# Squares over two score steps, score buffers as rows of one tile, and another order of the opening, in an attention and expert kernel on one core

## The chip, the core and the metric

The kernel runs on one core of a Trainium2 chip. The core has a matrix engine (TensorE: PE in the profile, its weight loads PEld), VectorE (DVE), ScalarE (ACT), GpSimd (POOL) and SyncE (SP), each with its own queue of instructions, taken in order; semaphores make one wait for another, and transfers run on 16 DMA engines. The metric is the time of one execution on the chip in microseconds.

## The reference

Attention without softmax over 8 batches, 12 heads, 448 positions and 64 columns a head, then a two-layer expert over the 3584 rows of 768 columns:

```python
scores = (1 / sqrt(64)) * q @ k.transpose(0, 1, 3, 2)
attn   = maximum(scores, 0) ** 2 / 448
x      = (attn @ v).transpose(0, 2, 1, 3).reshape(3584, 768)
h      = x @ w_in                                  # 768 -> 2048
out    = (0.5 * h * (1 + erf(h / sqrt(2)))) @ w_out    # 2048 -> 768
```

All arguments and the result are fp32. The kernel multiplies in bf16 and sums in fp32.

## The kernel before

**Stages of a batch.** The 12 heads of a batch are three groups g of four. Natural-layout loads (`add_k`, `add_q`, `add_v`, issued on POOL, L602, L511, L620, into `nk`, `nq`, `v_sb`) turn fp32 into bf16 on the way. Then K and Q are transposed into `kT` and `qT`: in batches 0 and 1 by TensorE through PSUM (L673 and the Q transposes beside it, with copies L563 on VectorE or L565 on ScalarE), from batch 2 on by DMA transposes issued on SP (`turn` in `add_T_dma`, L739). For each Q group a further step, the swap, writes it a second time with its two halves of partitions exchanged. The attention of one group takes seven *score steps* of 64 keys (`add_steps`): eight products of 64x64 tiles into a PSUM bank `ps` (L816); the relu with the scale into a bf16 buffer `a_sq` of 2 x 448 columns, on ScalarE (L828) or VectorE (L830); and the square, in place, on VectorE (L838). For the first group of batch 0 a score step covers half of the query columns of two key blocks, so it too has up to 896 columns, and the odd blocks at the end have 448. After seven squares comes the *attention product* (`add_av`, 28 products, L878, into `pav`), whose two halves are copied to `xT` by VectorE or ScalarE (L563, L565). The expert follows: six products into `psh` (L937, `add_f1`, the "expert product" of the text below), Gelu on ScalarE into `h_sb` (L947), and second-layer products, from batch 2 on mostly in a Strassen-like form whose sums of parts VectorE makes (L1089, L1120, L1266).

**Buffers.** The score buffers come from `apool`, a pool of `NA = 14` buffers; later in the kernel the same pool holds the fp32 parts of the Strassen-like form. PSUM has three banks of two for `ps` and `pav` (`banks`, class `Banks`) and two for `psh` and transposes (`f_pp`). `h_sb` is one tile, a ring for two batches, which is written and read in parts.

**The order.** A planner adds each operation with its engines, its dependencies and planned durations; its number is the order of its addition. Which engine takes it and in which place is written out by hand in the string `ORDER`. A word is a letter and a number: P is TensorE, A ScalarE, D VectorE, G GpSimd, S SyncE; `Z1056` is a filler of 1056 columns on TensorE, products with zeros that nobody reads. Each engine executes its words in the order of the string, whatever the others do. Since an engine takes its queue in order, an instruction that waits holds everything behind it.

**The opening.** Batch 0's group 0 is loaded first, by two fp32 loads from the ScalarE queue and one from SP's; `spin` and the filler keep TensorE at work until the data land. Then TensorE transposes and multiplies, and ScalarE and VectorE empty its banks, up to about 25 us, while batch 1's transposes and scores are mixed in.

**Holds.** POOL issues the loads, in the order of its queue. Between them stand *holds* (`add_gate`, L784): small POOL copies that read 16 columns of a transposed Q, so that POOL, and the loads behind it, waits until that transpose, or for batch 2 its swap, is done. There is one for each group of each batch from 2 to 6; the one of batch 2, group 1 is word `G224`:

```python
    def add_gate(b, g):
        def fn(e):
            nc.gpsimd.tensor_copy(gate, q_seg(b, 2 * g + (b == 2))[:, : SEG : SEG // 16])

        deps = [Tq[b, g, 0][b == 2]]
        pool_q.append(sch.add((("POOL", 0.2, 0.3),), fn, deps))
```

`qT` of batch b and of batch b + 2 lie in the same place, so a transpose for batch 4 may only be issued once batch 2's readers, the hold among them, are through.

Of the kernel before, what the change touches and what calls it, by code (L numbers as in the profile page):

```python
# [16 lines left out]
HS = S // 2  # L17
KB = 64
NK = S // KB
NA = 14  # L20
NN = 4
# [73 lines left out]
P127 A58 A102 D91 P129 P143 D94 D100 D103 P158 A144 A159 P104 A105 A106 G132 P146 D130 D147 D128  # L95
S213 P229 P170 P182 D183 G9 A230 P155 A171 D154 A156 P227 G114 P140 A141 D160 P194 P164 D165 A195
A228 P237 P149 P173 G131 P200 G134 P239 A238 P241 D145 A150 A201 A174 D148 D157 A240 P176 A177 D151
D142 D172 P161 D184 A162 A242 D166 P179 P167 P235 P233 D175 D178 D163 D180 P197 P206 G118 A168 A236
D169 A198 D181 A234 P185 D207 P203 A186 P188 P231 A187 A232 P243 D214 G221 P247 A244 S212 A248 D202
D204 P249 A250 P245 D189 A246 P257 P272 D199 D205 P191 P269 D192 A258 A273 A270 G117 P255 A256 D190  # L100
G138 P251 P266 D196 D193 S215 P275 A276 D208 S216 D267 A252 P209 A210 P281 P284 A211 P356 P340 A282
G133 D217 D285 P290 P305 P308 D291 D292 A357 P342 G137 G260 A341 A309 P344 G259 G136 D283 D306 A343
A345 P253 P299 P293 P278 D268 D286 D279 D280 D271 A254 P350 A351 P352 A353 P358 A359 S219 D220 P346
A347 D300 D301 D277 P362 A363 P366 P364 P302 D294 S218 D274 D295 P317 D303 P287 A318 A367 P329 P296
A365 A288 D310 A330 D304 D307 D289 D297 P360 A361 P354 A355 G222 P370 G223 G225 G261 P326 S389 D390
P314 A315 P332 D333 A327 P372 P323 S388 P320 G262 A321 G264 A371 D380 D298 P311 P439 S392 D324 D328
D322 D381 P430 P368 D383 A373 D384 A312 D334 D313 D316 A369 P348 A349 P338 A431 A339 P377 D382 A378
D385 A440 P411 S395 A412 G139 P445 D387 G226 A446 D325 D441 D407 G399 D386 P436 D331 D408 P433 P374
A375 A437 A434 P415 G263 G403 D393 D409 S391 P413 P457 P460 A461 S379 D319 D414 P335 P442 D458 P451
A336 A416 A452 P417 P419 D459 A443 A337 S394 D432 D396 D447 D418 D410 P454 P463 D420 P427 A428 P421  # L110
P423 P475 G265 D435 D553 D438 A455 A464 D429 P466 D444 G398 P448 D424 A476 D467 D422 G400 D456 G405
P478 P484 P521 G404 G397 G402 G224 A485 D479 D462 D468 D477 A449 P525 D465 D453 A522 S532 A450 P469
P481 D533 A526 P487 A488 A470 P511 A482 S531 P517 P493 D471 P490 S538 P472 D494 D495 D483 S535 A491
A512 G540 D473 G401 A518 D474 P606 P594 P529 A607 A595 P519 A530 P597 P591 P603 A520 P527 D551 D552
D489 A604 D480 D605 A528 G545 P501 A502 P513 A514 D592 D608 D598 S534 P505 A506 G542 P507 P600 D492
D593 P609 D486 P496 A610 D536 A508 A497 D601 G406 A498 P627 P630 D631 P523 A628 D602 A524 S537 S539
P615 P618 P633 P503 P509 D632 A619 G548 D611 A634 A504 D635 P515 D629 A510 D596 P499 P621 D599 A616
S376 A500 A622 P624 G541 D625 P612 A516 A613 S696 D620 P657 D614 D617 D626 P645 A658 S702 G550 P555
A646 A556 G544 D554 S426 S695 P557 P559 D697 S425 D623 P757 S699 G710 P639 P636 A758 D640 G547 P648
D558 A560 P760 D637 A761 P561 A638 P563 D641 D562 G708 D700 G705 D659 P654 A649 D650 G706 P772 P651  # L120
A773 D564 D571 A655 P565 A652 D566 D573 D572 P567 D568 P766 P754 P642 A643 A767 D656 G546 G549 S698
G709 P575 D653 D644 P577 P769 D774 D768 D647 S701 A576 A755 P778 A779 D770 D762 P660 P763 G712 P790
A764 A661 A791 P579 D578 S569 P581 D756 P787 P793 D771 D574 A580 A662 P796 A794 A797 D582 D765 D780
D792 A788 P583 S703 D759 D584 D789 P585 P808 G543 G707 S827 P802 A803 P775 P784 S829 G842 D809 P781
D586 P587 P669 S826 D795 D828 A782 D783 G837 A776 A777 D798 A785 D714 A670 P805 S830 P814 A815 D786
D806 S833 P799 P811 D810 D588 P817 S831 S570 D800 D801 D804 P667 A818 P671 A812 A668 P870 A871 D807
P867 P873 D816 D874 A868 P677 A672 P876 P820 P864 D819 A678 P691 A692 A877 P689 G711 P673 D875 D872
D821 D715 G838 S832 P891 D813 A865 D822 D892 G840 G713 P894 P823 A690 P879 D824 A895 A674 D896 P900
A880 P665 A825 D834 P663 G843 G839 D866 A901 G835 G836 G704 P882 P888 A666 D869 A664 P903 A889 A883
P683 S937 S940 A684 D893 P687 P693 P927 D717 D878 A904 S942 P897 D881 D884 A928 P885 P906 D898 A688  # L130
A694 S943 D907 P921 P679 S941 S590 A680 P685 S939 D899 D716 P681 A686 P675 A922 A682 D908 D902 A676
P718 D905 P918 A886 A887 P912 D890 P909 D919 P924 A913 D938 S936 P930 P720 D914 A719 D923 P722 A931
D925 A910 P915 P964 S589 A911 P952 D721 D926 D723 P724 A965 P726 D932 P985 D953 D920 D725 A916 D944
P946 P988 A947 D727 D734 P728 A986 A989 D735 D929 D917 P730 G841 P961 P955 D731 S733 D729 P933 A962
D736 P958 A956 A959 P738 D963 D934 A935 P949 A950 D737 P1009 P994 D960 D954 D948 D957 A739 P740
P742 D741 S732 D990 A995 A1010 G945 P744 P973 D951 D1028 D966 D996 D1011 P1006 A1007 A743 D745
D1026 D1018 P967 P997 A974 A998 P746 D846 D968 D1021 A969 D747 P748 P976 D749 D1027 A977 P982 P979
A980 A983 P750 D978 D844 P848 P970 D751 P1003 D845 P1000 P850 D981 D987 D999 A849 P852 D1008 D851
P854 A1004 D984 A1001 D975 P1012 A971 D972 D1005 S752 D1029 D1118 D1002 A1013 A853 D1014 P991 D855
D1022 D1023 P1015 D1019 D847 A992 A993 P856 A1016 A1017 P1064 A1065 D1324 P858 P1081 A1082 P1066  # L140
P1030 P1047 A1048 D1230 D1025 D1067 D1024 D1119 D1121 P1032 P1085 P1051 A1086 D857 A1052 P1070
P1049 P1068 D1231 A1069 A1031 P1055 D1050 D1033 P1053 D1054 D1071 D1020 P1072 D1073 P860 P1034
A1035 P1058 D1059 P1075 D859 P1156 P1036 P1078 D1056 P1061 D1076 D1322 D1062 D1037 P1122 P1083
A1157 P1160 A1123 A1161 P1089 D1079 D1084 D1232 D1120 P1041 D1042 P1158 A1074 P1038 A1080 P1087
P1139 A1077 P1126 A1127 A1140 D1039 D1088 D1090 A1091 D1159 P1092 P1095 P1173 A1060 A1174 P1162
A1043 D1093 P1044 D1045 P1124 D1096 D1125 D1163 P1177 P1143 A1097 A1057 A1046 A1178 P1141 D1142
P1128 P1130 P1175 S862 A1094 A1040 D1129 P1145 P1167 D1176 S753 D1131 A1144 D1168 P1179 A1063 D1098
P1285 A1169 D1146 P1147 D1148 P1136 D1180 D861 P1150 D1151 P1102 P1133 D1134 P1184 D1099 D1137
D1100 D1185 P1164 D1165 P1153 P1181 P1104 P1234 A1132 D1154 A1286 A1149 A1103 D1105 D1182 A1186
P1268 P1106 P1170 P1108 A1107 A1152 P1110 D1109 D1171 D1101 D1111 S863 A1235 P1289 P1187 A1135  # L150
D1190 D1191 A1166 D1188 P1251 P1114 D1115 S1117 A1183 A1252 P1255 P1112 A1172 P1194 P1253 P1236
D1113 A1138 A1269 P1272 D1193 D1192 A1155 D1237 A1189 A1290 A1273 P1196 D1254 P1238 P1287 P1240
D1195 P1198 A1239 D1197 D1199 P1200 P1270 D1233 D1288 D1271 D1201 A1256 P1293 P1257 P1291 P1242
P1202 D1258 D1241 P1274 D1243 D1292 P1296 D1203 P1245 P1248 P1204 D1249 D1246 D1294 D1275 P1262
D1205 P1326 D1210 P1276 D1297 A1298 A1327 D1211 P1206 P1279 D1280 D1277 D1212 D1207 P1259 P1330
D1260 P1214 P1282 P1299 D1300 P1216 P1377 S1209 A1215 D1323 D1263 P1328 D1329 P1360 A1247 D1217
P1265 A1295 A1361 A1264 P1332 P1218 D1266 D1283 A1219 A1284 S1116 D1325 D1213 A1278 P1220 A1281
P1334 P1222 D1221 D1223 P1224 P1364 P1226 A1331 A1267 D1225 A1301 P1306 P1362 D1304 D1302 D1303
D1333 P1337 D1227 P1379 D1335 P1340 A1378 D1363 D1380 A1307 A1244 P1366 P1310 D1341 D1338 P1383
# [272 lines left out]
def kernel(  # L432
# [366 lines left out]
    def add_steps(todo, bias=0.0, dve=False):  # L799
        for blocks in todo:  # L800
# [58 lines left out]
            for blk in blocks:  # L859
                if blk[2] == NK - 1:  # L860
                    add_av(blk, bias)
# [777 lines left out]
```

## Time and profile before

| | |
|---|---|
| three runs | 364.56, 364.74 and 364.97 us, median 364.74 |
| profiled execution, its span | 364.6 us |
| TensorE busy | 354.6 us, 97% |
| VectorE busy | 297.8 us, 82% |
| ScalarE busy | 205.5 us, 56% |
| GpSimd busy | 67.0 us, 18% |
| granted TensorE clock in the slices of the span | 9 tenths or more in all of them |

The profile is of one execution. Its own time and its span are the same 364.6 us, as there is one core and the span runs from its first to its last instruction; the runs have their median 0.1 us above that. In a group of instructions the columns are line, engine, operation, output and inputs by the program's names, shapes, count, then busy time and mean duration, then the idle time of the engine just before them and what ended most of it. A line of a timeline has the start, the length, the engine and the work, with the idle time before it in brackets.

### The profile page before, as it was taken

What the parts mean: (1) busy time and instruction counts of PE and PEld (TensorE: products, weight loads), DVE (VectorE), ACT (ScalarE), POOL (GpSimd) and SP (SyncE); (2) the same over time, 40 slices, a digit from 0 to 9 for tenths busy, and PEclk for the clock granted to TensorE, in tenths of its full rate; (3) what the DMA queues carried; (4) which work ended last, traced back from release to release, by engine and by line L of the source; (5) the groups of instructions that cost most, each with busy time, mean ns of one, the idle gap of its engine ahead of it and who ended that gap; (6) DMA issues with size and microseconds to landing.
All of it is one profiled execution on the core that took longest, in us unless ns stands there. A gap on an engine that the chain in (4) does not pass through costs nothing.

```text
span 364.6 us, 8274 instructions
## 1 busy us (share of the span) xinstructions
PE 354.6 (97%) x3439; PEld 222.0 (61%) x3439; DVE 297.8 (82%) x510; ACT 205.5 (56%) x333; POOL 67.0 (18%) x102
## 2 busy tenths in 40 slices
PE   8799999999999899999999999999999999999995
PEld 4464544555544455554455555899977887787663
DVE  3999878869999779999977999987866576767764
ACT  4999665546678585777966766425634025235000
POOL 8666173111723024052000000000000000000000
PEclk9999999999999999999999999999999999999999
DMA  9999999999899999999955301020101002402324
GB/s 175 201 200 200 184 172 178 191 197 207 134 173 177 144 232 166 196 173 224 192 132 72 91 2 45 2 62 27 42 6 43 2 8 80 131 0 61 99 58 131
DMA packets 72085, 43.87 MB, mean 120 GB/s; under 512 B 36336, under 2 KB 68720, under 8 KB 72048
## 3 DMA queue, kind: packets, MB, share of 16 engines
q0 software_dynamic: 32032, 22.47, 42.8%
q1 hardware_dynamic: 39120, 20.03, 28.6%
q10 hardware_dynamic: 896, 0.85, 0.7%
q8 instruction: 27, 0.44, 0.5%
q14 instruction: 10, 0.08, 0.1%
HBM read 45.61 MB, written 11.01 MB: 155 GB/s over the span
## 4 chain that ended last, share of the span: by engine, by line
PE 63%; DMA 21%; DVE 5%; ACT 4%; issue 3%; POOL 2%; SPq 0%; POOLq 0%; DVEq 0%
PE pso L1266 27%; PE pb L1089 18%; DMA nq<-in_q_dram 9%; PE psh L937 7%; DMA qT<-nq 7%; PE ps L816 5%; PE pav L878 4%; ACT a_sq L828 4%; DMA kT<-nk 4%; DVE a_sq L838 2%; DMA nk<-in_k_dram 2%; PE spin L1445 1%; DVE osb L1300 1%; DVE qT L563 1%; POOL wout_sb L532 1%
## 5 line engine op out<-in xcount | busy, mean ns | idle before, releaser
L828 ACT ACTIVATE a_sq<-ps 128x896 bf16<-128x896 f32 x126 | 110.5, 925 | 36.5 <-PE ps L816 36.2
L838 DVE TENSOR_TENSOR a_sq<-a_sq 128x896 bf16<-128x896 bf16 x169 | 96.4, 615 | 2.0 <-ACT a_sq L828 1.6
L937 PE MATMUL psh<-xT,win_sb 128*128 128x448 bf16 x384 | 76.9, 353 | 0.0
L830 DVE TENSOR_SCALAR a_sq<-ps 128x896 bf16<-128x896 f32 (+1 forms) x43 | 46.2, 1076 | 15.9 <-PE ps L816 15.6
L937 PEld LDWEIGHTS <-win_sb 128*128 128x128 bf16 x384 | 35.6, 98 | 38.2 <-issue 7.2
L1120 DVE TENSOR_TENSOR part<-pb,part 128x448 f32<-128x448 f32 x80 | 46.9, 619 | 12.9 <-PE pb L1089 11.1
L1266 PEld LDWEIGHTS <-s_sb 128*128 128x128 bf16 x424 | 40.4, 98 | 27.1 <-issue 3.3
L816 PE MATMUL ps<-qT,kT 64*64 64x448 bf16 (+1 forms) x700 | 47.8, 350 | 3.6 <-ACT a_sq L828 1.9
L947 ACT ACTIVATE h_sb<-psh 128x448 bf16<-128x448 f32 x64 | 34.5, 549 | 19.5 <-PE psh L937 19.5
L1266 PEld LDWEIGHTS <-h_sb 128*128 128x128 bf16 x312 | 29.9, 98 | 20.1 <-issue 2.3
L1089 PEld LDWEIGHTS <-win_sb 128*128 128x128 bf16 x384 | 36.9, 98 | 2.2
L1266 PE MATMUL pso<-t_sb,s_sb 128*128 128x384 bf16 x208 | 38.1, 326 | 0.0
L1266 PE MATMUL pso<-wout_sb,h_sb 128*128 128x384 bf16 x208 | 38.1, 326 | 0.0
L1266 PE MATMUL pso<-wout_sb,s_sb 128*128 128x384 bf16 (+1 forms) x208 | 37.7, 324 | 0.2 <-DVE osb L1300 0.2
L878 PE MATMUL pav<-a_sq,v_sb 64*64 64x448 bf16 (+1 forms) x700 | 36.1, 342 | 1.2 <-ACT a_sq L828 0.8
L1132 ACT ACTIVATE h_sb<-part 128x448 bf16<-128x448 f32 x48 | 25.2, 573 | 21.1 <-DVE part L1120 21.1
L816 PEld LDWEIGHTS <-kT 64*64 64x64 bf16 x700 | 18.3, 105 | 26.6 <-issue 18.1
L1300 DVE TENSOR_TENSOR osb<-pso,p_sb 128x384 f32<-128x384 f32 x39 | 21.5, 552 | 13.5 <-PE pso L1266 10.9
L878 PEld LDWEIGHTS <-v_sb 64*64 64x64 bf16 x700 | 20.9, 107 | 12.7 <-issue 2.2
L1089 PEld LDWEIGHTS <-ws 128*128 128x128 bf16 x288 | 27.7, 98 | 1.2
L1089 PE MATMUL pb<-xs,ws 128*128 128x224 bf16 x192 | 22.8, 259 | 0.0
L1089 PE MATMUL pb<-xs,win_sb 128*128 128x224 bf16 x192 | 22.5, 259 | 0.0
(70 smaller groups left out, 311.8 us busy)
## 6 DMA issues: line engine op xcount, KB each, us to landing
nk<-in_k_dram POOLq DMA_DIRECT2D x23, 224.0 KB, 8.1
nq<-in_q_dram POOLq DMA_DIRECT2D x23, 224.0 KB, 8.8
v_sb<-in_v_dram POOLq DMA_DIRECT2D x4, 672.0 KB, 8.9
out_dram<-osb SPq DMA_DIRECT2D x7, 336.0 KB, 3.8
v_sb<-in_v_dram POOLq DMA_DIRECT2D x10, 224.0 KB, 8.0
out_dram<-osb SPq DMA_DIRECT2D x7, 288.0 KB, 2.8
out_dram<-osb SPq DMA_DIRECT2D x8, 240.0 KB, 3.3
win_sb<-in_moe_w_in_dram POOLq DMA_DIRECT2D x8, 192.0 KB, 9.0
```

Source lines behind the costliest of these rows:

```text
L816: nc.tensor.matmul(ps[64 * j : 64 * j + 64, e, x * w : x * w + w], kT[r, g, i * 128 + 64 * j : i * 128 + 64 * j + 64], moving, start=True, ...
L828: A.activation(ar, ps, AF.Relu, scale=c_att)
L830: V.tensor_scalar(ar, ps, c_att, 0.0, op0=mybir.AluOpType.mult, op1=mybir.AluOpType.max,)
L838: V.tensor_mul(box["a2"][:, :, :used], ar, ar)
L878: nc.tensor.matmul(pav[0][o2 : o2 + 64, e, :w], get_v()[r, 2 * v_slot(b, g) + e, bass.ts(i, D)], box["a2"][r, y, o : o + w], start=(i == 0 ...
L937: nc.tensor.matmul(ph[:, x * n : x * n + n], win_sb[:, kd, bass.ts(m + x, 128)], xT[b][:, kd, c], start=(kd == 0), stop=(kd == KD - 1),)
L947: A.activation(h_ring()[:, m : m + nm, o + c.start : o + c.stop], box[0][:, :S].rearrange("p (x n) -> p x n", x=nm), AF.Gelu,)
L1089: nc.tensor.matmul(ps[name][:, z * HS : z * HS + HS], w[:, k, bass.ts(mm, 128)], right()[:, k], start=first and k == 0 and z == 0, stop=k ...
L1120: V.tensor_add(get(to), ps[name][:, :S], get(other))
L1132: A.activation(h_ring()[:, m : m + 2, o + half[c].start : o + half[c].stop], src().rearrange("p (x n) -> p x n", x=2), AF.Gelu,)
L1266: nc.tensor.matmul(box[bank][:, n0:n1], left()[:, kf], right()[:, kf, n0:n1], start=bool(need) and kf == 0, stop=kf == K2 - 1, skip_group_ ...
L1300: V.tensor_add(out()[:, n0:n1], box[bank][:, n0:n1], other()[:, n0:n1])
```

## The change

Four things are changed together.

1. In batches 0 and 1 (`PAIRED = 2`) the score steps of a group are taken in pairs. The two relus write into one buffer of up to 2 x 896 columns, and one square covers both; the seventh step has a square of its own. So a group has four squares in place of seven, and a square waits for two relus.
2. The 14 score buffers are now 14 rows of one tile (`Slots`), handed out when the kernel is built: the row, or pair of rows, that was given back longest ago. A row is given back by the attention product that reads it. For the Strassen-like form the tile is opened anew with rows of fp32.
3. In the written order the hold of batch 2, group 1, moves up on POOL: `G224` before, `G205` now, from behind the load `G402` to a place ahead of the load `G139` (now `G129`).
4. The opening stands in another order, on all engines, and some of its relus and copies change between ScalarE and VectorE; the filler moves from its start to a place between score steps. TensorE's order differs from before up to about the first score steps of batch 4, and is the same from there to the end.

Numbers shift, since paired squares are fewer operations: those behind batch 0's squares are 10 lower, those behind batch 1's 19 lower (`P627` is now `P608`). The order of SP's queue is the same. POOL's differs only in the hold.

```diff
-ORDER = """
-D13 G0 Z1056 A10 G1 G7 G4 A16 G108 G1461 P11 D12 P14 D15 P17 P29 P32 D18 P38 D39 P19 P21 A30 D20
-P35 D22 P27 A33 P62 D31 P77 A36 D40 D28 A63 P59 D34 P44 P25 G2 G3 A78 A60 D37 D45 G111 P121 P65 A66
-P71 A72 P47 P74 A75 D79 A48 D122 D64 D67 P23 D73 P50 D24 D26 P68 G107 P41 A51 P98 A69 D76 A99 D61
-D52 D70 P53 P123 G5 G115 G112 A42 A43 G8 G116 A54 G6 P95 P86 A96 A87 P80 D46 D124 A81 A82 P89 P92
-P119 D55 D97 D49 D90 P125 P83 A93 A84 D120 P56 G109 G110 G113 P152 D126 D88 G135 D85 A57 A153 P101
...
+ORDER = """
+A10 D13 G0 G1 G7 G4 G98 G1442 P11 P14 A16 A15 D12 P17 P31 A18 P29 P19 P34 P21 A30 A20 D32 D35 A22
+P36 P27 P70 P55 D28 D33 A37 A71 A56 P42 P65 P25 P57 D43 G2 G3 A66 A58 G101 P60 Z1056 P44 P62 A45 P23
+P67 G97 D26 D38 D61 A63 A68 P39 P49 P47 G5 G105 G102 A40 A24 A41 A48 D59 D64 D69 D50 D72 D51 D46 G8
+G106 G6 P109 P86 P111 P88 P73 A87 A110 A89 A112 A74 P83 P81 P115 P113 D82 D75 A84 D85 D116 A114 P76
+P78 P91 A77 A79 A92 G99 G100 G103 G125 P145 P119 P117 P140 P52 A146 A141 A53 A54 D80 D90 D93 P94 A95
...
+class Slots:
...
+    def open(self, dtype, size):
+        assert not self.held
+        self.size = size
+        self.tile = self.pool.tile([128, self.n * size], dtype, tag="a", name="a_sq")
+
+    def take(self, k=1, near=0):
+        busy = {y for x, c in self.held.values() for y in range(x, x + c)}
+        runs = []
+        for x in range(0, self.n, k):
+            if not busy & set(range(x, x + k)):
+                alone = near if k == 1 and x ^ 1 not in busy else 0
+                runs.append((alone + max(self.used.get(y, 0) for y in range(x, x + k)), x))
+        x = min(runs)[1]
+        t = self.tile[:, x * self.size : (x + k) * self.size]
...
-    apool = pool("apool", NA)
+    apool = pool("apool", 1)
...
+    slots_a = Slots(apool, NA, 2 * S)
...
+        for _, steps in runs:
+            n = 2 if steps[0][0][0] < PAIRED else 1
+            for x in range(0, len(steps), n):
+                add_pair(steps[x : x + n], bias, dve)
...
-            def fn_relu(e_, box=box, used=used):
-                box["a2"] = apool.tile([128, 2, S], BF16, tag="a", name="a_sq")
-                ar, ps = box["a2"][:, :, :used], box["ps"][:, :, :used]
+            def fn_relu(e_, n=n, used=used, off=off):
+                if "a" not in box:
+                    box["a"] = slots_a.take(len(steps), 6 if steps[0][0][0] < PAIRED else 0)
+                ar = box["a"][:, off : off + 2 * used].rearrange("p (y n) -> p y n", y=2)
+                ps = box["ps", n][:, :, :used]
...
-            def fn_mul(e_, box=box, used=used):
-                ar = box["a2"][:, :, :used]
-                V.tensor_mul(box["a2"][:, :, :used], ar, ar)
...
+        def fn_mul(e_, total=total):
+            ar = box["a"][:, :total]
+            V.tensor_mul(ar, ar, ar)
...
+        o3 = sch.add((("DVE", d, d + 0.12),), fn_mul, relus, bias=bias)
...
+            for box in {id(SQ[x][1]): SQ[x][1] for x in blocks}.values():
+                slots_a.give(box["a"])
...
-                tmp[name] = apool.tile([128, S], F32, tag="a", name="part")
+                if slots_a.size > S:
+                    slots_a.open(F32, S)
+                tmp[name] = slots_a.take()
```

More of the change, by code (lines that the diff above doesn't have):

```diff
@@ L20 @@
 NA = 14
+PAIRED = 2
 NN = 4
@@ L110 @@
[L110 to L119, printed above, removed]
@@ new lines @@
+G106 G6 P109 P86 P111 P88 P73 A87 A110 A89 A112 A74 P83 P81 P115 P113 D82 D75 A84 D85 D116 A114 P76
+P78 P91 A77 A79 A92 G99 G100 G103 G125 P145 P119 P117 P140 P52 A146 A141 A53 A54 D80 D90 D93 P94 A95
+D118 D120 A96 G122 P142 P130 P210 P166 D143 D131 A211 A167 S194 P208 P135 P137 P132 P218 G9 G104
+A133 A209 D144 D168 D136 D147 A138 A219 D134 P156 P151 P220 P222 P177 G121 G124 A152 A157 A178 D139
+P158 P148 P182 A221 A149 D159 D160 D150 A183 A223 P153 P214 P163 P161 P216 A215 D162 D154 A164 A217
@@ new lines @@
+S200 P343 P345 P289 S199 D201 D267 D252 D288 D255 D282 D258 D290 A344 A346 P310 P268 P298 P347 P335
+D299 A269 A348 A270 D311 D300 A336 G203 G204 G206 G242 P295 P313 P307 P351 P341 S370 A314 D285 D291
+D273 D276 D361 A352 A296 A308 A342 S369 P353 P349 P304 P292 G243 G245 G205 A354 A350 D362 D363 D315
+D371 D305 S373 P301 P426 P358 D293 A294 A427 A302 A359 D364 D365 D297 P417 P411 P420 P329 P319 S376
+G129 G207 G380 A412 A330 A320 A418 A421 D306 D309 D366 D303 D368 D413 D312 D367 D374 D388 D389 D377
@@ new lines @@
+P584 P468 P510 P500 A454 D458 D461 D455 D585 D586 D467 A469 A511 A501 G526 P578 P474 P581 P488 P482
+A579 A489 S515 G523 P508 A582 A483 A509 D475 D464 D470 D473 D574 D583 D517 D476 D533 G387 P494 P486
+P575 P608 A495 A487 A609 D576 S518 S520 P477 P611 P590 P504 G529 A591 D478 D612 D613 D610 D592 D534
+D580 A479 A505 P484 P490 P599 P596 P614 A485 A491 P480 P496 A600 A615 D577 D616 A597 D589 P602 S357
+A481 A603 P605 G522 D606 P593 A497 A594 S677 D601 P638 D595 D598 D607 P626 A639 S683 G531 P536 A627
@@ L168 @@
+D1388 A1368 D1395 D1390 A1340 P1391 D1396 D1392 P1399 D1397 S1394 D1400 P1401 P1403 A1357 S1393
+D1398 D1402 D1404 P1405 P1407 D1406 D1408 P1409 D1415 D1417 D1410 P1411 D1416 D1412 P1419 S1414
+D1420 P1421 D1422 P1423 D1424 P1425 S1436 S1413 P1427 D1418 P1433 D1426 D1428 D1431 D1435 S1437
+S1440 P1429 P1432 D1430 S1438 D1434 S1439
 """
@@ L428, in give, with __init__ @@
             self.free.append(self.slot[id(t)][0])
+class Slots:
+    def __init__(self, pool, n, size):
+        self.pool, self.n, self.size = pool, n, size
+        self.used, self.clock, self.held = {}, 0, {}
+        self.open(BF16, size)
+    def open(self, dtype, size):
[11 more added lines that the diff above has]
+        t = self.tile[:, x * self.size : (x + k) * self.size]
+        self.held[id(t)] = (x, k)
+        return t
+    def give(self, t):
+        x, k = self.held.pop(id(t))
+        self.clock += 1
+        for y in range(x, x + k):
+            self.used[y] = self.clock
 @with_exitstack
@@ L799, in add_steps, with add_pair, fn_qk @@
     def add_steps(todo, bias=0.0, dve=False):
+        runs = []
         for blocks in todo:
-            box = {}
+            key = (blocks[0][:2], blocks[0][3])
+            if not runs or runs[-1][0] != key:
+                runs.append((key, []))
+            runs[-1][1].append(blocks)
+        for _, steps in runs:
+            n = 2 if steps[0][0][0] < PAIRED else 1
+            for x in range(0, len(steps), n):
+                add_pair(steps[x : x + n], bias, dve)
+    def add_pair(steps, bias, dve):
+        box, relus, sizes = {}, [], []
+        for n, blocks in enumerate(steps):
             w = S if blocks[0][3] is None else HS
             used = w * len(blocks)
-            def fn_qk(e_, blocks=blocks, box=box, w=w):
-                ps = box["ps"] = banks.take("ps")
+            off = sum(sizes)
+            sizes.append(2 * used)
+            def fn_qk(e_, blocks=blocks, n=n, w=w):
+                ps = box["ps", n] = banks.take("ps")
                 for x, (b, g, i, half) in enumerate(blocks):
@@ L833, in fn_relu @@
                     )
[L834 to L838 removed]
+                banks.give(box["ps", n])
             deps = []
@@ L851, in add_steps @@
             o2 = sch.add(
-                eng, fn_relu, [o1], need=("a",), frees=("w",), bias=bias, other=RELU_DVE
-            )
-            d = 0.07 + used / 960
-            o3 = sch.add((("DVE", d, d + 0.12),), fn_mul, [o2], bias=bias)
-            for x, blk in enumerate(blocks):
-                QK[blk] = o1
-                SQ[blk] = (o3, box, x * w)
-            for blk in blocks:
-                if blk[2] == NK - 1:
-                    add_av(blk, bias)
+                eng, fn_relu, [o1], need=() if n else ("a",) * len(steps), frees=("w",),
+                bias=bias, other=RELU_DVE,
+            )
+            relus.append(o2)
+            for blk in blocks:
+                QK[blk] = o1
+        total = sum(sizes)
+        def fn_mul(e_, total=total):
+            ar = box["a"][:, :total]
+            V.tensor_mul(ar, ar, ar)
+        d = 0.07 + total / 1920
+        o3 = sch.add((("DVE", d, d + 0.12),), fn_mul, relus, bias=bias)
+        for n, blocks in enumerate(steps):
+            w = S if blocks[0][3] is None else HS
+            for x, blk in enumerate(blocks):
+                SQ[blk] = (o3, box, sum(sizes[:n]) + x * w, sizes[n] // 2)
+        for blk in steps[-1]:
+            if blk[2] == NK - 1:
+                add_av(blk, bias)
     def add_av(blk, bias):
@@ L876, in fn @@
                         n, y = (i, e) if b < 2 else divmod(NK * e + i, 2)
-                        _, box, o = SQ[blocks[n]]
+                        _, box, o, used = SQ[blocks[n]]
+                        o += y * used
                         nc.tensor.matmul(
@@ L884, in fn @@
                         )
+            for box in {id(SQ[x][1]): SQ[x][1] for x in blocks}.values():
+                slots_a.give(box["a"])
         deps = list(dict.fromkeys(SQ[x][0] for x in blocks)) + ld_v[b, g]
-        last = {id(SQ[x][1]): x for x in SQ}
-        gone = sum(last[id(SQ[x][1])] == x for x in blocks)
+        gone = sum(len(o.deps) for o in {id(SQ[x][0]): SQ[x][0] for x in blocks}.values())
         d = 7 * 0.19 * w / S
@@ L1138, in fn @@
                     banks.give(ps["a"])
+                if frees == ("a",):
+                    slots_a.give(src())
             d = 0.19 + 0.00069 * S
```

121 lines of the change are left out of this document (56 added, 65 removed).

## The prediction

> **What bounds the kernel now.** I read the page first, then the busy times by stretch, the list of waits, the chain, and last the timelines of single engines. From the page, and from the table of stretches (window, its length, then busy time and count of PE, PEld, DVE, ACT, POOL):
>
> ```profile
> span 364.6 us, 8274 instructions
> PE 354.6 (97%) x3439; PEld 222.0 (61%) x3439; DVE 297.8 (82%) x510; ACT 205.5 (56%) x333; POOL 67.0 (18%) x102
> ...
> 10.00:15.00 5.00, 3.69 (x86) 2.31 (x86) 5.00 (x10) 4.91 (x7) 2.73 (x4) 1.00 1.26 203
> 15.00:20.00 5.00, 3.91 (x79) 2.39 (x82) 4.80 (x10) 5.00 (x10) 3.52 (x5) 1.00 1.39 196
> 20.00:25.00 5.00, 4.84 (x132) 3.64 (x125) 4.98 (x9) 5.00 (x9) 3.66 (x7) 1.00 1.30 200
> 120.00:140.00 20.00, 18.69 (x186) 9.40 (x187) 15.33 (x26) 12.96 (x22) 5.43 (x9) 1.00 1.17 194
> 240.00:300.00 60.00, 60.00 (x542) 51.99 (x540) 45.14 (x82) 21.86 (x46) 0.00 (x0) 1.00 0.09 28
> ```
>
> TensorE sets the end: whoever wants to shorten the run must remove its idle time, and there is little. Two places matter here. From 10 to 25 us TensorE has 2.6 us idle while VectorE and ScalarE are full: the opening is bound by these two, which empty PSUM. Between 120 and 140 us it loses 1.3 us at once. What waits, from the timelines of PE and SP, the waits of SP's queue, and POOL's timeline:
>
> ```profile
> 123.20 1.49 PE L878 MATMUL pav<-a_sq,v_sb 64*64 64x448 bf16 x28
> 126.01 0.57 PE L816 MATMUL ps<-qT,kT 64*64 64x448 bf16 x8 [1.31 <-DMA kT<-nk]
> ...
> 43.78 9.94 SPq L739 DMA_TRANSPOSE qT<-nq  x2
> ...
> 90.01 2.22 SPq L739 DMA_TRANSPOSE kT<-nk  x1
> 97.70 1.31 SPq L739 DMA_TRANSPOSE qT<-nq  x1
> ...
> SPq L739 <- POOL gate L784: 5.3, 1, 5.3
> ...
> 71.53 0.22 POOL L784 COPY gate<-qT 128x16 bf16<-128x16 bf16 x1
> 96.73 0.72 POOL L511 DMA_DIRECT2D nq<-in_q_dram  x1
> 97.45 0.22 POOL L784 COPY gate<-qT 128x16 bf16<-128x16 bf16 x1
> 106.74 0.24 POOL L784 COPY gate<-qT 128x16 bf16<-128x16 bf16 x1 [9.07 <-DMA qT<-nq]
> 107.25 0.70 POOL L602 DMA_DIRECT2D nk<-in_k_dram  x1 [0.27 <-issue]
> ```
>
> At 126.01 the first score step of batch 4, group 1 waits for its transposed K. That K was loaded at 107.25, behind the hold at 106.74 (a hold is the small POOL copy that waits for a transpose, so that the loads behind it wait too), which waited 9.07 us for the Q transpose issued at 97.70. SP was through with the transpose before it at 92.2 (90.01 + 2.22) and then stood 5.3 us for POOL: the new transpose writes over batch 2's Q buffer, which the hold at 97.45 still had to read. That hold is the one for batch 2, group 1, G224 of the order. The chain confirms the leg:
>
> ```profile
> 97.70 8.92 DMA qT<-nq
> 106.76 0.49 issue
> 107.25 5.71 DMA nk<-in_k_dram
> 112.98 12.98 DMA kT<-nk
> 126.01 0.57 PE ps L816 x8
> ```
>
> **The hold that moves.** As G205 it now stands ahead of the load of V of batch 2, group 2 (G129), which ran right before the hold at 71.53, so at about 71 us. It passes eight loads and three holds on POOL; their order is kept. The swap that it waits for belongs to a Q transpose issued from 43.78 on, so it costs the 0.22 us of its copy and saves the same later. SP's next Q transpose then goes at about 92.4. It takes between 5.1 us (another Q transpose, in the fence below) and 8.9 us (its own row), so it lands at 97.5 to 101.3. POOL is busy until 97.45, so the K load leaves between 97.8 and 101.6, 5.6 to 9.4 us before 107.25, and transposed K lands near 117 to 120 if the remaining 18.8 us stay. TensorE needs it at 124.5, as worked out below; so the 1.3 us of idle go, and nothing else of the DMA chain is late next. The later loads move forward too and share the rings; up to 5 us of that are covered.
>
> **The squares.** Batch 0 goes from 22 to 12 squares and batch 1 from 21 to 12: 19 fewer on VectorE. Rows of DVE and ACT, first by shape (busy us, mean ns), then stretches of the timelines (start, length), then two lines of the chain:
>
> ```profile
> L838 DVE TENSOR_TENSOR a_sq<-a_sq 128x896 bf16<-128x896 bf16 x167 | 95.7, 617 | 2.0 <-ACT a_sq L828 1.6
> L830 DVE TENSOR_SCALAR a_sq<-ps 128x896 bf16<-128x896 f32 x42 | 45.5, 1086 | 15.5 <-PE ps L816 15.2
> L1195 DVE TENSOR_TENSOR t_sb<-wout_sb,t_sb 128x1536 bf16<-128x1536 bf16 x4 | 3.7, 954 | 0.0
> L563 DVE COPY kT<-tp 128x896 bf16<-128x896 bf16 x5 | 3.1, 616 | 0.0
> L828 ACT ACTIVATE a_sq<-ps 128x896 bf16<-128x896 f32 x125 | 110.1, 927 | 36.5 <-PE ps L816 36.2
> L828 ACT ACTIVATE a_sq<-ps 128x448 bf16<-128x448 f32 x1 | 0.7, 657 | 0.0
> L565 ACT CAST xT<-pav 128x448 bf16<-128x448 f32 x26 | 13.3, 540 | 0.9 <-PE pav L878 0.6 <-DVE xT L563 0.2
> ...
> 5.90 0.39 PE L673 MATMUL tp<-ident,nk 128*128 128x128 bf16 x4
> ...
> 23.16 3.29 DVE L838 TENSOR_TENSOR a_sq<-a_sq 128x896 bf16<-128x896 bf16 x6
> ...
> 7.32 10.93 ACT L828 ACTIVATE a_sq<-ps 128x896 bf16<-128x896 f32 x13 [1.59 <-PE ps L816]
> 27.16 0.97 ACT L565 CAST xT<-pav 128x448 bf16<-128x448 f32 x2
> ...
> 27.30 1.24 PE psh L937 x6
> ...
> 84.78 5.14 DMA qT<-nq
> ```
>
> Six squares in a row take 3.29 us: one occupies VectorE for (3.29 - 0.617) / 5 = 0.535 us. From 896 to 1536 columns the duration rises by 0.337 us, 0.527 ns a column; 1792 columns make 1.09 us, or 1.01 of occupancy, against 2 x 0.535 = 1.07. A pair saves 0.06 us, 19 pairs 1.1 us, and the ten of the opening 0.6 us. All of it is VectorE's; it reaches the end only where VectorE is last. In return a square waits for both of its relus.
>
> **The opening's other order.** This is what decides. Moved from VectorE to ScalarE: six transposes' copies of 896 columns (A20, A22, A24, A110, A112, A114; before D20, D22, D24, D120, D122, D124), the first two K pieces (A15, A18; 512 and 384 columns) and the 448-column relu A37. Moved the other way: the relus of 896 columns D32, D35, D61, the 448-column D50, and one attention copy (D75). A relu of 896 columns occupies ScalarE for (10.93 - 0.93) / 12 = 0.83 us, a cast of 448 for 0.97 - 0.54 = 0.43, a relu of 448 about 0.5. The trace has no ScalarE copy of a bf16 transpose. Its bounds: 0.43 us if ScalarE took two bf16 elements at a time, as VectorE does (a copy 0.53 us, a relu from f32 1.0), and 0.83 if it takes one, like every ScalarE row there is. I take 0.83. So ScalarE gains 6 x 0.83 + 0.9 + 0.5 = 6.4 us and loses 3 x 0.83 + 0.5 + 0.43 = 3.4, and one batch-1 relu fewer stands ahead of batch 0's last attention copies (0.83): 2.1 us more up to them.
>
> The Trainium skill, "ScalarE: Activation LUTs", section "Step-by-step: what each stage is for", says that ScalarE takes one element per cycle, 0.833 ns, for fp32 and bf16 alike. By it a copy of 896 columns streams in an estimated 0.75 us, six in 4.5 instead of 5.0, and the sum ahead would be 0.5 us less; no row here shows a bf16 source, and the rule speaks against this move, since VectorE does the same copy in 0.53.
>
> ScalarE ran from 7.32 without a real gap to 28.13 (27.16 + 0.97). Its first K copy can now start when the transposes end, 6.3, so 1.0 us earlier, with some 0.2 of new waits before the first score. Batch 0's last copies end 2.1 - 1.0 + 0.2 = 1.3 us later, and with them the first expert products, which fill TensorE from 27.30 on. VectorE is relieved of nine pieces and stands idle meanwhile. Bounds: with 0.43 a copy, 2.4 us less on ScalarE, VectorE becomes the end and the opening is about 0.2 us shorter (its saved squares against waits of about 0.4); with longer waits at the start, 2.0 us longer. After the opening TensorE is full and the delay stays in its queue.
>
> **Smaller edits.** The 1056-column fill moves from 5.13 us into the opening, between score steps: 0.45 us where TensorE waits anyway, 0.45 lost if not. One tile in place of fourteen buffers costs nothing if reads and writes of different rows do not wait for each other: the h_sb ring is written and read by parts in one tile, and its writer waits for its own product alone:
>
> ```profile
> ACT h_sb L947 <- PE psh L937: 19.5, 32, 1.4
> ACT a_sq L828 <- PE ps L816: 36.2, 37, 2.6
> ...
> 126.58 1.24 PE psh L937 x6
> 128.51 4.65 PE psh L937 x24
> ```
>
> The relus wait for scores only, never for a free buffer, so pairs that hold two rows at once have room. Up to the order's P602 (before P621, started 133.09) TensorE does the same work in another sequence, and from there its order is unchanged. The sequence has four more changes between kinds of product: six products alone take 1.24 us, in a row 4.65 / 4 = 1.16, so 4 x 0.08 = 0.3 us. The first step that needs the late K (P608, before P627) now stands ahead of the attention product P477 and one score step, 1.5 us of work: TensorE, free at 126.01 - 1.31 = 124.7 before, reaches it at 124.7 - 1.5 + 1.3 = 124.5.
>
> **Sum**, against the profiled execution's span: 364.6 + 1.3 (opening) - 1.3 (126 us) + 0.3 = 364.9. The three runs have their median at 364.74, 0.1 above this span: 365.0. About 0.2% (0.7 us) is what a measurement can tell from no change.
>
> **Rivals.** *The opening costs nothing* (faster). If ScalarE copies bf16 at double rate, or its extra work lies where it would have waited, the opening is between 0.2 shorter and 0.2 longer, and 126 us pays: 365.0 - 1.3 = 363.7, down to 363.3. For it: ScalarE idles 1.59 us before 7.32, and VectorE has the shorter queue. Against: ScalarE is at 5.00 of 5 us until 25. *The K is still late* (slower). The loads that leave earlier crowd the rings, and K lands at 126 again. TensorE now arrives with 1.5 us of work undone, waits there until 126 as before, and still has it to do, with some 0.2 of the switches: 364.7 + 1.5 + 0.2 = 366.4. It decides from a landing after 124.5 on. For it: that transpose took 12.98 us behind five loads. Against: the chain gains at least 5.6 us. *Rows wait for each other* (the change does not do what it says): if a relu waited for the attention products of other rows, 16 of the 24 products would each stop ScalarE for 1.3 us, over 10 us more. The h_sb row speaks against it.
>
> **Chances.** Forecast 0.54, of which 0.34 within 0.2%, 0.14 slower (opening longer by 2.0 rather than 1.3) and 0.06 faster; opening free 0.22; late K 0.21; rows 0.03. So faster 0.28, same 0.34, slower 0.38. The range runs from the free opening at its best, 363.3, to the late K, 366.4, and leaves out the tails beyond.
>
> **What would show it.** Right: SP's wait for the gate gone, a Q transpose at about 92.4, no wait for kT at the batch-4 step; 24 squares in batches 0 and 1 at about 1.09 us for 1792 columns; ScalarE copies of kT and qT near 0.93 us; the first expert product at 28.6 instead of 27.30, VectorE with idle time before 30. Wrong: ScalarE copies near 0.55 us, the first expert product at or before 27.3, or a kT wait that stays.

## The result, and the profile after

The changed kernel takes 367.06 us (median of 7; 366.69 to 370.78), the kernel before 364.74 (median of 7, same chip): a ratio of 1.0074, interval 1.0051 to 1.0097. It is slower by 2.3 us; forecast were 365.0 and a range up to 366.4.

The spans of these executions are given beside their times, and a time is always 1.7 to 1.9 us more than its span. So the statement above that the profiled execution's time and its span are the same 364.6 us is wrong: with this span it was an execution of some 366.4 us. The profiled execution of the change, 370.78 us, is the slowest of its seven, so a second profile was taken of each kernel. First the page of the change, first profile:

```profile
span 369.0 us, 8260 instructions
PE 355.6 (96%) x3439; PEld 221.7 (60%) x3439; DVE 294.5 (80%) x487; ACT 209.3 (57%) x337; POOL 64.8 (18%) x102
```

VectorE has 3.3 us less and ScalarE 3.8 more to do than before. The table of stretches (window, length, then busy time and count of PE, PEld, DVE, ACT and POOL, granted clock, DMA share, GB/s) of the second profile of before, and of the second of the change:

```profile
core 0 of [0], span 363.6 us
...
10.00:15.00 5.00, 3.88 (x88) 2.36 (x89) 5.00 (x10) 4.91 (x7) 3.18 (x5) 1.00 1.27 204
15.00:20.00 5.00, 3.62 (x84) 2.24 (x79) 5.00 (x11) 5.00 (x9) 2.71 (x5) 1.00 1.36 191
20.00:25.00 5.00, 4.77 (x116) 3.29 (x114) 4.78 (x10) 5.00 (x9) 3.57 (x6) 1.00 1.32 203
```

```profile
core 0 of [0], span 365.1 us
...
10.00:15.00 5.00, 4.00 (x81) 2.56 (x84) 4.67 (x7) 4.97 (x8) 2.41 (x4) 1.00 1.26 203
15.00:20.00 5.00, 4.14 (x114) 2.90 (x107) 5.00 (x7) 5.00 (x9) 3.43 (x5) 1.00 1.38 196
20.00:25.00 5.00, 3.13 (x64) 1.81 (x58) 3.86 (x5) 5.00 (x8) 3.72 (x7) 1.00 1.31 204
```

Between 20 and 25 us TensorE now stands for 1.9 us of the 5, while ScalarE is full and VectorE is not. What it waits for there, from the timelines of PE, ACT and DVE of the change (second profile):

```profile
22.44 1.10 PE L865 MATMUL ps<-qT,kT 64*64 64x448 bf16 x12 [0.20 <-DVE a_sq L881]
24.54 0.38 PE L865 MATMUL ps<-qT,kT 64*64 64x448 bf16 x4 [1.00 <-ACT a_sq L879]
...
18.95 1.04 ACT L599 COPY kT<-tp 128x896 bf16<-128x896 bf16 x1
19.74 1.07 ACT L879 ACTIVATE a_sq<-ps 128x896 bf16<-128x896 f32 x1
20.55 1.06 ACT L599 COPY qT<-tp 128x896 bf16<-128x896 bf16 x1
21.33 0.71 ACT L599 CAST xT<-pav 128x448 bf16<-128x448 f32 x1
21.76 1.11 ACT L879 ACTIVATE a_sq<-ps 128x896 bf16<-128x896 f32 x1
22.57 1.10 ACT L599 COPY kT<-tp 128x896 bf16<-128x896 bf16 x1
23.35 4.38 ACT L879 ACTIVATE a_sq<-ps 128x896 bf16<-128x896 f32 x5
...
25.33 2.63 DVE L910 TENSOR_TENSOR a_sq<-a_sq 128x1792 bf16<-128x1792 bf16 x3 [0.80 <-ACT a_sq L879]
```

Score steps have filled their three banks by 23.5 us; the bank that TensorE wants at 24.5 waits for a relu on ScalarE, and ahead of that relu stand copies of transposed K and Q. VectorE idles 0.8 us for a later relu of the same row of five. The whole way, from the first transposes to the step from which TensorE's order is the same again (P621 before, P602 after), by the first and last rows in PE's timelines, with the first expert product between them, before and after (second profiles):

```profile
6.74 0.37 PE L705 MATMUL tp<-ident,nq 112*128 112x112 bf16 x4
...
28.28 1.31 PE L937 MATMUL psh<-xT,win_sb 128*128 128x448 bf16 x6
...
132.81 0.57 PE L816 MATMUL ps<-qT,kT 64*64 64x448 bf16 x8
```

```profile
5.58 0.37 PE L739 MATMUL tp<-ident,nq 112*128 112x112 bf16 x4 [0.48 <-ACT nq L599]
...
28.80 0.55 PE L998 MATMUL psh<-xT,win_sb 128*128 128x448 bf16 x2
...
134.16 0.57 PE L865 MATMUL ps<-qT,kT 64*64 64x448 bf16 x8
```

That is 126.07 us before and 128.58 after, 2.5 more. Of this, 1.7 lie in the opening, up to the first expert product: 28.28 - 6.74 = 21.5 us before, 28.80 - 5.58 = 23.2 after. It is 21.5 in each trace with the opening of before, apart from the one with a moved copy, and 23.2 in each trace of the change with its own opening. Behind the first expert product the two run the same products, TensorE never stands idle in either trace, and the change takes 0.8 us more, so the sequence alone costs that: 104.53 us in all five traces with TensorE's order of before and no wait there, 105.36 to 105.37 in three with that of the change. Leaving out the filler, TensorE's order changes 71 times between transposes, attention and expert products on the whole way, before 59 times; behind the first expert product it changes 51 times, before 43 times.

The 1.7 us of the opening are mostly waits: between the first transposes and 30 us, TensorE runs no product for 3.3 us before and for 4.6 to 4.7 in the traces of the change. The filler's products also lie in this stretch now, from 12.68 us on, and were ahead of it before. The next wait behind them, 0.38 us at 13.88, is again for a relu, so they may fill time in which TensorE would have waited; no run has the change without them.

Against it stands the start: the transposes begin at 5.58 instead of 6.74, as the filler no longer stands ahead of them. With the filler ahead they began at 5.69, 6.74, 6.82, 6.82, 6.02 and 6.65 in six traces; with it moved, between 5.46 and 5.66 in all.

### The profile page after: what moved, and what is told of

The parts are those of the page before. It is cut to its first block, busy times and chain, and to the rows that moved or that the text cites. A ratio compares the mean times of both kernels' runs of the same rounds, so it can differ in the third digit from the quotient of the medians.

```text
span 369.0 us, 8260 instructions
## 1 busy us (share of the span) xinstructions
PE 355.6 (96%) x3439; PEld 221.7 (60%) x3439; DVE 294.5 (80%) x487; ACT 209.3 (57%) x337; POOL 64.8 (18%) x102
## 4 chain that ended last, share of the span: by engine, by line
PE 75%; DMA 12%; DVE 6%; ACT 4%; issue 1%; POOL 1%; DVEq 0%; POOLq 0%
PE pso L1331 30%; PE pb L1150 17%; PE psh L998 12%; PE ps L865 7%; PE pav L938 7%; DMA kT<-nk 4%; DMA nk<-in_k_dram 3%; DMA qT<-nq 3%; ACT a_sq L879 2%; DVE a_sq L910 2%; DMA nq<-in_q_dram 2%; PE pso L1437 1%; DVE qT L597 1%; ACT kT L599 1%; DVE s_sb L1310 1%
## 5 line engine op out<-in xcount | busy, mean ns | idle before, releaser
L879 ACT ACTIVATE a_sq<-ps 128x896 bf16<-128x896 f32 x126 | 111.8, 935 | 26.8 <-PE ps L865 26.0
L910 DVE TENSOR_TENSOR a_sq<-a_sq 128x896 bf16<-128x896 bf16 (+2 forms) x150 | 94.8, 676 | 2.8 <-ACT a_sq L879 2.3
L998 PE MATMUL psh<-xT,win_sb 128*128 128x448 bf16 x384 | 77.8, 353 | 0.0
L1183 DVE TENSOR_TENSOR a_sq<-pb,a_sq 128x448 f32<-128x448 f32 x80 | 46.9, 619 | 12.9 <-PE pb L1150 11.1
L1331 PEld LDWEIGHTS <-s_sb 128*128 128x128 bf16 x424 | 40.4, 98 | 27.2 <-issue 3.3
L1195 ACT ACTIVATE h_sb<-a_sq 128x448 bf16<-128x448 f32 x48 | 25.2, 573 | 21.1 <-DVE a_sq L1183 21.1
```

The costliest lines, as they stand in the source:

```text
L879: A.activation(ar, ps, AF.Relu, scale=c_att)
L910: V.tensor_mul(ar, ar, ar)
L998: nc.tensor.matmul(ph[:, x * n : x * n + n], win_sb[:, kd, bass.ts(m + x, 128)], xT[b][:, kd, c], start=(kd == 0), stop=(kd == KD - 1),)
L1183: V.tensor_add(get(to), ps[name][:, :S], get(other))
L1195: A.activation(h_ring()[:, m : m + 2, o + half[c].start : o + half[c].stop], src().rearrange("p (x n) -> p x n", x=2), AF.Gelu,)
L1331: nc.tensor.matmul(box[bank][:, n0:n1], left()[:, kf], right()[:, kf, n0:n1], start=bool(need) and kf == 0, stop=kf == K2 - 1, skip_group_ ...
```

## The experiments

Every row is against runs of before on the same chip; the ratio has its 95% interval beside it.

| kernel | median us | before | ratio, interval |
|---|---|---|---|
| before, again | 365.19 | 365.06 | 0.9996, 0.9980 to 1.0011 |
| before, hold moved | 365.66 | 365.06 | 1.0025, 1.0004 to 1.0046 |
| the same, again | 365.27 | 365.34 | 1.0016, 0.9995 to 1.0037 |
| change, hold moved back | 367.18 | 365.06 | 1.0063, 1.0042 to 1.0083 |
| rows of one tile only | 365.10 | 365.06 | 1.0004, 0.9989 to 1.0018 |
| change, squares not paired | 367.26 | 365.04 | 1.0066, 1.0045 to 1.0088 |
| change, eight copies on VectorE | 370.68 | 365.04 | 1.0154, 1.0136 to 1.0172 |
| change, one copy on VectorE | 366.26 | 365.04 | 1.0036, 1.0022 to 1.0050 |
| before, that copy on ScalarE | 366.33 | 365.04 | 1.0037, 1.0022 to 1.0051 |
| change, again | 366.90 | 365.17 | 1.0064, 1.0040 to 1.0088 |
| change, both engines rearranged | 365.90 | 365.17 | 1.0032, 1.0016 to 1.0048 |
| the same, hold moved back | 365.79 | 365.34 | 1.0019, 1.0009 to 1.0029 |

**The kernel before, once more.** No edit.

> The kernel before, unchanged, for a second profile and for the spans of many executions. Theory A (the wait of 1.3 us at 126 us belonged to the one profiled execution, which was an execution of about 366.4 us): the spans are about 1.8 us below the times, near 363.0, as they are for the changed kernel, and a second profile shows the wait at the batch-4 score step shorter or gone in some executions. Theory B (the wait is there every time): spans near 364.6 and the same wait of 1.3 us.

Theory A. Of the 29 executions of before beside this kernel's, 27 have spans from 362.3 to 365.1 us (the other two took 370.44 and 1280.63), and the one with a span of 364.6, like that of the profile on which the prediction stands, took 366.45. In the second profile the score step at the disputed place follows the attention product without a wait (124.25 + 1.49 is past the start of the next line, as the rows of the two overlap):

```profile
124.25 1.49 PE L878 MATMUL pav<-a_sq,v_sb 64*64 64x448 bf16 x28
125.58 0.72 PE L816 MATMUL ps<-qT,kT 64*64 64x448 bf16 x8
```

**The hold alone.**

```diff
-A412 G139 P445 ... G397 G402 G224 A485
+A412 G224 G139 P445 ... G397 G402 A485
```

> The kernel before with the one hold G224 moved ahead of the load G139, nothing else. Theory A: 364.7, no change (within 0.3), as there is no wait to remove in most executions. Theory B, the prediction's: 1.3 us less, 363.4. Theory C (the earlier loads crowd the DMA rings of batch 2's transposes): slower by 0.5 or more, with waits for kT between 50 and 80 us.

No gain: 365.66 and, the second time, 365.27. Theory B falls. The first median lies 0.6 over before, more than theory A allows and as theory C has it, but the trace has no wait for kT, and the second time nothing of it was left. What the move did to the chain of loads, from the timelines of SP and POOL, first of before (second profile), then with the hold moved:

```profile
98.74 1.27 SPq L739 DMA_TRANSPOSE qT<-nq  x1
...
107.06 0.21 POOL L784 COPY gate<-qT 128x16 bf16<-128x16 bf16 x1 [8.35 <-DMA qT<-nq]
107.58 0.70 POOL L602 DMA_DIRECT2D nk<-in_k_dram  x1 [0.31 <-issue]
```

```profile
93.44 4.30 SPq L739 DMA_TRANSPOSE qT<-nq  x1
...
105.98 0.21 POOL L784 COPY gate<-qT 128x16 bf16<-128x16 bf16 x1 [10.61 <-DMA qT<-nq]
106.49 0.70 POOL L602 DMA_DIRECT2D nk<-in_k_dram  x1 [0.31 <-issue]
```

The transpose was issued 5.3 us sooner, as foretold, and took 12.5 us in place of 8.3 up to the hold that waits for it, so that the K load came only 1.1 us sooner, and no product waited for it.

> The kernel before with the moved hold alone, once more, for more executions beside those of the first time (median 0.6 over before, one of 12 at 368.63). Theory H: again single executions 1 us or more above the median, and a median 0.1 to 0.6 over before. Rival: none, and a median within 0.2 of before.

The median is that of before; two of its twelve executions lie 3.3 and 3.4 us above it, so the first half of theory H holds and the second doesn't.

**The change with the hold back.**

```diff
-P304 P292 G243 G245 G205 A354 ... G385 G378 G383 D430
+P304 P292 G243 G245 A354 ... G385 G378 G383 G205 D430
```

> The changed kernel with the hold G205 back behind the load G383, its old place. Theory A: 367.1, no change. Theory B: 1.3 us more, 368.4, with a wait of about 1.3 us or more for kT at the batch-4 step. Theory C: less than 366.7, and no waits for kT between 50 and 80 us.

367.18: no change, theory A.

**Rows of one tile only.** The code of the change with `PAIRED = 0` and the order of before.

> The changed kernel's code with no pairs and the order of before: only the 14 buffers become rows of one tile. Theory A: 364.7, as before, within 0.3. Rival (rows wait for each other, or the rows are handed out in another sequence that makes a relu wait for a reader): over 366, with ScalarE or VectorE waits before relus that name the attention product.

365.10. The rows wait for nothing that the buffers didn't.

**The change without pairs.** `PAIRED = 0` again, with the order of the change, each pair's two squares one behind the other in its place.

> The changed kernel with every square on its own again, each pair of squares in the place of the paired one; order, engines and rows as in the change. Theory A (the order and the division between ScalarE and VectorE cost the 2 us, the pairs are neutral): 2.0 to 2.4 us over before, as the change. Theory P (pairs make squares wait for a second relu, and that costs it): within 0.7 us of before. Theory Q (pairs save 1.1 us on VectorE and this reaches the end): 3.4 us over before.

367.26, as the change. The opening takes the same 23.2 us. Pairs neither cost nor bring anything that shows: P and Q fall.

**Eight copies to VectorE.**

```diff
-A16 A15 D12 P17 P31 A18 ... A20 ... A22 ... A24 ... A110 ... A112 ... A114
+A16 D15 D12 P17 P31 D18 ... D20 ... D22 ... D24 ... D110 ... D112 ... D114
```

> The changed kernel with all eight copies of transposed K and Q (A15, A18, A20, A22, A24, A110, A112, A114) given to VectorE, in the same places of the order. Theory A1 (ScalarE's total alone is the bound of the opening): 6 us of work leave ScalarE, so the 1.7 us of the opening go and it is 0 to 0.7 us over before. Theory A2 (both engines are full, and a copy behind squares in VectorE's queue comes later than on ScalarE): 1 to 2 us slower than the change, 3.3 to 4.3 over before.

370.68, 5.6 over before: A1 falls, A2 has the sign and is too small. PE's timeline and the stretches:

```profile
9.40 0.39 PE L746 MATMUL tp<-ident,nq 112*64 112x112 bf16 x8
11.67 0.77 PE L865 MATMUL ps<-qT,kT 64*64 64x448 bf16 x16 [1.88 <-DVE qT L597]
...
10.00:15.00 5.00, 2.70 (x44) 1.64 (x44) 4.33 (x7) 2.61 (x4) 2.74 (x4) 0.81 1.28 203
15.00:20.00 5.00, 4.20 (x95) 2.74 (x87) 4.58 (x7) 4.20 (x7) 3.15 (x5) 0.85 1.37 197
20.00:25.00 5.00, 3.79 (x86) 2.44 (x81) 5.00 (x9) 3.73 (x5) 3.92 (x6) 1.00 1.31 202
25.00:30.00 5.00, 4.30 (x66) 2.80 (x67) 5.00 (x7) 3.35 (x4) 2.62 (x4) 0.67 1.30 201
```

Now VectorE is the engine that is late, ScalarE has room, and the granted clock falls to 0.81, 0.85 and 0.67 in three of the stretches. The opening takes 26.9 us. How much of that is the clock's is not known.

**One copy, both ways.** The copy of K of batch 0, group 2.

```diff
-A40 A24 A41          (the change)      -D73 P50 D24 D26      (before)
+A40 D24 A41                            +D73 P50 A24 D26
```

> The changed kernel with one copy alone, that of K of batch 0, group 2 (A24, the one between the two attention copies at 16 us), on VectorE in its place. Theory A1 and A2: one ScalarE copy of 0.81 us less ahead of the stretch at 20 to 25 us where score steps wait for ScalarE: 0.6 to 0.8 us faster than the change, 1.4 to 1.7 over before. Theory P, or a cost of the order on TensorE alone: no change, 2.1 over before.

> The kernel before with the same one copy (D24) on ScalarE in its place. Theory A: ScalarE has no gap from 7 to 28 us, so its 0.81 us are added: 0.6 to 0.9 over before. Theory P, or a cost of TensorE's order alone: no change, within 0.2 of before.

In the change, the copy's move to VectorE makes it 366.26, 1.2 over before instead of 2.1; in before, its move to ScalarE costs 1.3. In the trace of the latter the opening is 0.8 us longer (22.3 for 21.5), the width of one ScalarE copy; in that of the former it is only 0.3 shorter, with a new wait of 0.69 us for VectorE ahead of the attention product at 19.5. Both medians moved further than the openings, and that of before further than the 0.6 to 0.9 foretold; the change came out below its 1.4 to 1.7. The rest lies within the intervals. The sign is theory A's in both.

**The change once more, and with both engines rearranged.** The second kernel leaves TensorE's order, pairs, rows, filler and hold as they are. The first words of the queues of ScalarE and VectorE:

```diff
-A 10 16 15 18 30 20 22 37 71 56 66 58 45 63 68 40 24 41 48 87 110 89 112 74 84 114 77
+A 10 16 15 18 32 35 22 28 71 43 66 58 45 63 68 40 50 41 48 87 89 74 84 75 82 77
-D 13 12 32 35 28 33 43 26 38 61 59 64 69 50 72 51 46 82 75 85 116
+D 13 12 30 20 37 33 38 56 26 61 59 72 24 64 69 110 112 46 114 51 85 116
```

> The changed kernel, unchanged, for a second profile. Theory A: its waits for transposed K at 51 to 56 and at 75 us belonged to that execution; this profile has a span near 365.3, none of these waits of over 0.3 us, and the lost 1.7 us in the opening again. Rival (the moved hold makes them): they are there again, and the span is over 367.

> The changed kernel with TensorE's order, the pairs, the rows, the filler and the hold as they are; only words of ScalarE and VectorE of the opening change: five copies of transposed K and Q (A20, A24, A110, A112, A114) and four relus (A30, A37, A56 and, later, the places of a few squares) go to VectorE, six relus (D32, D35, D43, D50, D82 and two of batch 1), one copy of Q (D28) and one attention copy (D75) to ScalarE, in the places that a walk through the queues with the measured durations finds best. Theory A2 (the division between the two engines and their order of service cost the opening 1.7 us): 1.8 to 2.1 less than the change, 0 to 0.4 over before. Rival (TensorE's other order, with its pairs, costs it): no more than 0.5 less than the change.

The change again: 366.90, span of its profile 365.1, none of the late waits, and the opening 23.2 us again. Rearranged: 365.90, 1.0 less than the change, and 0.7 over before. From the first transposes to P602 its trace takes 127.37 us (the change 128.58), and the opening 21.9 instead of 23.2. The table of stretches:

```profile
15.00:20.00 5.00, 4.55 (x122) 3.06 (x112) 5.00 (x7) 4.90 (x9) 3.30 (x5) 1.00 1.39 200
20.00:25.00 5.00, 3.93 (x92) 2.58 (x96) 4.14 (x7) 5.00 (x8) 3.76 (x6) 1.00 1.29 200
```

So 1.3 of the opening's 1.7 us come back when only the division between the two engines and their order change, with TensorE's order, pairs and rows as they were. The theory had asked for 1.8 to 2.1 and its rival for no more than 0.5; the 1.0 lies between. That the remaining 0.3 of the opening belong to TensorE's order is not shown, as another division might win them too; behind the first expert product this kernel takes about as long as the change (105.5 us and 105.4).

> The kernel with the rearranged opening, and the hold back in its old place as well. So far 8 of 54 executions with the moved hold lay 1.1 us or more above the median of their kernel, and none of 36 without it. Theory H (the moved hold makes the late transposes of these executions): no execution more than 1 us above the median, and a median of 365.4 to 365.9, 0.2 to 0.7 over before. Rival (chance, or TensorE's other order): single executions at 367 and above remain, about one in seven.

365.79: the hold is worth nothing here either. One execution, at 367.04, lies 1.2 us above its median, so theory H isn't shown.

**What stays open.** Executions 1.1 us or more above their kernel's median were 10 of 66 with the moved hold and 4 of 127 without it (among the latter, the runs of before beside the other kernels, two of 609.67 and 1280.63 us left out). That speaks for a connection. But in the first profile of the change, which is such an execution, what TensorE waits for was late before the moved hold ran at 65.90 us. The K of the last wait below was loaded from 48.53 on, and its transpose was issued at 61.26, against 54.30 in the second profile:

```profile
51.78 0.76 PE L865 MATMUL ps<-qT,kT 64*64 64x448 bf16 x12 [0.60 <-DMA kT<-nk]
55.59 1.52 PE L938 MATMUL pav<-a_sq,v_sb 64*64 64x448 bf16 x28 [1.50 <-DMA v_sb<-in_v_dram]
75.11 0.38 PE L865 MATMUL ps<-qT,kT 64*64 64x448 bf16 x4 [1.56 <-DMA kT<-nk]
...
40.00:60.00 20.00, 17.91 (x167) 8.29 (x160) 13.54 (x17) 12.56 (x22) 7.09 (x10) 1.00 1.44 134
```

The DMA engines were busier there (1.44) and moved less (134 GB/s; 1.28 and 199 in the second profile). These three waits, 3.7 us, are the distance between that execution and the median. The profile of the change without pairs, an execution of 369.11 us with a median of 367.26, has the same: waits of 0.52 us for a load of V at 53.93 and of 1.40 for a transposed K at 73.29, whose load left at 48.37 and whose transpose at 59.31, ahead of the hold at 63.87. Why it happened is not known.

## Why the prediction was wrong

**The base and the hold: failed.** The sum began at the profiled span, 364.6, as if that were the execution's own time, 0.1 from the median. The execution took some 1.8 us more than its span and so some 1.7 more than the median, and the wait of 1.3 us at 126 us, which the second profile lacks, was the largest part of that. So the hold was credited with -1.3 us for removing a wait that the median execution doesn't have; moved alone, it gained nothing. Without this term the same sum gives 364.7 + 1.3 + 0.3 = 366.3. The second half of the step failed too: of the 5.3 us by which the transpose left sooner, 1.1 reached the K load, not 5.6 to 9.4, because the transpose took 12.5 us, beyond the 5.1 and 8.9 between which it was put. Why it took longer is not known.

**The opening: right in mechanism, too small.** ScalarE is the engine that is late, and it is late for the reason given: copies of transposes ahead of relus. The first expert products began at 28.7 and 28.8 us, against 28.6 forecast (before: 27.2 and, with the later start, 28.3). That is close in part because the change starts earlier; from the first transposes on, the opening grew by 1.7 us, not 1.3. The sum priced the delay of batch 0's last copies. It left out the score steps of batch 1 that wait for banks behind the same copies (1.00 us at 24.54), and the filler's products in this stretch; which of the two makes the 0.4 us is not shown. The price of a copy was right. In its queue the copy of 896 bf16 columns occupies ScalarE for 19.74 - 18.95 = 0.79 us, between which and 0.83 little lies. The Trainium skill, "ScalarE: Activation LUTs", section "Step-by-step: what each stage is for", gives one element per cycle for bf16 as for fp32, an estimated 0.75 us for these columns, and the trace agrees.

**The switches: mis-sized.** Twelve more changes between kinds of product, not four; the eight of them behind the first expert product go with 0.8 us there, and the sum had 0.3 for all.

**The filler: its sign was missed.** It was put at nothing, or at 0.45 us lost. At the start it had cost up to 1.2 us (5.66 with slow first products and the filler moved, up to 6.82 with it ahead), so that its move gives some of the opening's loss back.

**The squares and the rows: right.** A square of 1792 columns takes 1.09 us as forecast, VectorE has the time saved, and none of it shows in the time: without pairs the change takes as long. No row waits for another.

**The sum of what was measured:** 364.7, plus 1.7 of opening and 0.8 of sequence, less the earlier start, which is 0 to 1.2 us by the execution, is 366.0 to 367.2; the 367.06 measured lies near its upper end. Of the rivals, "the opening costs nothing" is refuted by its 1.7 us, "the K is still late" by the traces without a wait for it, and "rows wait" by the kernel that has only the rows.

## What to carry to other kernels

Before a wait in a profile is credited to an edit, set the profiled execution's own time beside the median, and take a second profile: a wait that sets off a slow execution from the others isn't there to be gained. Where two engines empty PSUM and both are full, moving work between them is worth what the later of the two loses at each place, copy by copy: one copy cost 1.3 us in one place, and eight moved at once to the other engine cost 3.5. A transfer that is issued 5 us sooner into busy DMA queues may land 1 us sooner, as the Q transpose here did.

## What the runs showed of the hardware

With all eight copies on VectorE, TensorE's waits in the opening grew to as much as 1.88 us, and the granted clock, 1.00 in every stretch of the other traces' openings shown here, fell to 0.67 in one stretch. Products then run slower as well: the filler's two of 512 columns took 1.05 us there (from 15.23) and 0.59 in the change (from 12.68). That the waits brought the clock down is not shown by a run of its own. And the last six of the products with zeros at the start, 512 columns each, took 2.0 us in some executions and 2.77 in others, with the filler behind them at 0.64 or 1.0:

```profile
3.10 2.77 PE L1445 MATMUL spin<-zero 128*128 128x512 bf16 x6
5.80 1.00 PE L1601 MATMUL fill<-zero 64*64 64x512 bf16 x3
```

This is of before's second profile; the second of the change has 2.00 for the first line, and no filler there. These products start 0.43 us apart at first and 0.22 apart from some moment on, which came at about 4.2 us in the second profile of the change and, in before's, not before the last of them at 5.24. This makes about 1 us between executions of before.
